# A rebuilt first chunk, and three smaller edits, in a gated attention and feed-forward kernel

## The chip, the cores and the metric

The kernel runs on one core of one Trainium2 chip. A core has TensorE (PE, matrix multiplication), VectorE (DVE), ScalarE (ACT), GpSimd (POOL) and SyncE (SP), each with its own instruction queue, and 16 DMA engines that all queues share. The metric is the device time of one execution in microseconds (us), lower is better. Times of a profile count from the start of its span.

## What is computed

```python
def _attn_ref(u, v, z):            # u, v: (8, 3008, 256)   z: (8, 3008, 64)
    scale = 1.0 / S
    scores = scale * np.matmul(z, z.transpose(0, 2, 1))
    attn = np.maximum(scores, 0.0) ** 2
    out = np.matmul(attn, v)
    return (u * out).astype(np.float32)

def _moe_ref(x, w_in, w_out):      # w_in: (256, 2048)   w_out: (2048, 256)
    h = x @ w_in
    g = h * (1.0 / (1.0 + np.exp(-1.702 * h)))
    return (g @ w_out).astype(np.float32)
```

The second function is applied to the 24064 rows that the first one gives. The scores are symmetric, since z is multiplied with itself.

## The kernel before

The eight batches are done one after the other. In a batch the 3008 rows of the sequence are six chunks of 512 (the last of 448), and a chunk is four blocks of 128; there are 24 blocks, NJ, numbered j. For each chunk i the loop of `attend` (L283) runs over all blocks j and multiplies V block j (stationary) with the squared scores of block j against chunk i (moving, 512 columns), for both halves c of V's columns, into two accumulators "o" in PSUM.

The scores come in units (i, jp) of two blocks: two matmuls of ZT with ZT (`scores`, L208), a relu by ScalarE out of PSUM to f16 "rl", a square by VectorE to "a" (`square`, L225). ZT is z transposed, with its 64 features twice on the 128 partitions, so that the two matmuls of a unit can run side by side in two halves of the array. Because the scores are symmetric, only units on and above the diagonal are worked out; for those below, "a" is turned by a DMA transpose on SP's queue into a tile "tt" (L253). Those of chunk 0 in batches 1 to 7 with jp 6 to 9 aren't turned at once: they go to a list `late`, which is worked off after unit (1, 11).

The order of all five engines is written out by hand: instructions stand in each engine's queue in the order in which the code emits them. `sched[i]` says at which step n of chunk i how many units are taken from `queue` (`take`, L591). After the attention of a batch come the up-projection (`up_group`, L348, "hg" and the gelu), the down-projection of four chunks as products of a seven-product scheme (`products` and `product`, L432 and L440, "st", with left sums "s" made by VectorE) and of two chunks plainly (`down64`, L505, "yp"). The next batch's chunk 0 units are taken in the two `down64` loops. In the last batch all six chunks use the seven-product scheme, and 14 products are left over after the last up-projection group.

The start of batch 0 is of its own kind (L599 to L616). V's first four blocks come on ACT's queue and all of z on SP's queue (`first_z`), then the rest of V on SP's. Seven matmuls on zeros warm TensorE up. z comes in six groups g of four blocks: VectorE casts a group to f16 twice, side by side (`first_cast`, L124), TensorE transposes it in four pieces into "zp" (`first_zt`, L130), and one engine copies it to ZT, ScalarE for g 0, 2 and 3 (L136), VectorE for the others (L138). Groups 2 to 5 are transposed at steps 2, 7, 13 and 21 of chunk 0. GpSimd casts V from f32 to f16 (L173) in two instructions for four blocks.

In chunk 0 of batch 0, step n stands for V half n % 2 of block n // 2 up to block 18; the last blocks follow per half. 14 units are taken up to its end: 12 of chunk 0 and two of chunk 1. A unit's PSUM tile "sc" has two buffers, "rl" three, "a" 21, "tt" 14 (shared with other tiles), the o and zp tiles together four.

Of the kernel before, what the change touches and what calls it, by code (L numbers as in the profile page):

```python
# [9 lines left out]
F32 = mybir.dt.float32  # L10
F16 = mybir.dt.float16
P = 128
# [3 lines left out]
def kernel(  # L16
# [25 lines left out]
    CB = CH // P  # L42
    NU = NJ // 2
# [30 lines left out]
    nil = pw.tile([P, CH], F16, name="nil", tag="gf")  # L74
    dve.memset(nil, 0.0)

    late = []
# [15 lines left out]
    def warm_up(n):  # L93

        w = ps1.tile([P, CH], F32, name="w", tag="ps1")
        for k in range(n):
            pe.matmul(w, nil[:, :P], nil, start=(k == 0), stop=(k == n - 1))  # L97

    def first_z(cuts):


        ZT[0] = pz.tile([P, NJ, P], F16, name="ZT", tag="ZT")
        ZT["st"] = [pa.tile([P, CB * CB, 2, DQK], F16, name="zst", tag="tt", bufs=14) for _ in range(2)]
        fs = [pw.tile([P, CB * CB, DQK], F32, name="zf", tag="y") for _ in range(2)]
        for n0, n1 in zip(cuts, cuts[1:]):
            zf = fs[n0 // (CB * CB)]
            m0 = n0 % (CB * CB)
            t0, last = n0 * P, n1 == NJ
            t1 = (n1 - CB if last else n1) * P
            sp.dma_start(  # L110
                zf[:, m0:m0 + (t1 - t0) // P, :].rearrange("p (g n) d -> p g (n d)", n=CB),
                z[0, t0:t1].rearrange("(g p n) d -> p g (n d)", p=P, n=CB),
            )
            if last:
                m1 = m0 + (t1 - t0) // P
                sp.dma_start(zf[:, m1:m1 + CB - 1, :], z[0, t1:S0].rearrange("(p n) d -> p n d", n=CB - 1))
                for h in range(2):
                    sp.dma_start(zf[h * SREM:(h + 1) * SREM, m1 + CB - 1, :], z[0, S0:S])
        ZT["f"] = fs

    def first_cast(g):
        m = g % CB * CB
        for c in range(2):
            dve.tensor_copy(ZT["st"][g // CB][:, m:m + CB, c, :], ZT["f"][g // CB][:, m:m + CB, :])  # L124

    def first_zt(g):
        z2 = ZT["st"][g // CB][:, g % CB * CB:(g % CB + 1) * CB]
        zp = ps1.tile([P, CB, P], F16, name="zp", tag="ps1")
        for k in range(CB):
            pe.transpose(zp[:, k, :], z2[:, k, :, :], ident)  # L130
        zt = ZT[0][:, g * CB:(g + 1) * CB, :].rearrange("d n p -> d (n p)")
        nb = CB if g < NCH - 1 else CB - 1
        dst = zt[:, :nb * P].rearrange("d (p n) -> d p n", n=nb)
        src = zp[:, :nb, :].rearrange("d n p -> d p n")
        if g in (0, 2, 3):
            act.activation(dst, src, AF.Copy, scale=1.0)  # L136
        else:
            dve.tensor_copy(dst, src)  # L138
        if nb < CB:
            dve.tensor_copy(zt[:, nb * P:], zp[:, nb, :])  # L140


    def load_z(b):
        ZT[b] = pz.tile([P, NJ, P], F16, name="ZT", tag="ZT")
# [12 lines left out]

    def load_v(b, n0, eng):


        if n0 == 0:
            V16[b] = pz.tile([P, NJ, NCC, P], F16, name="V16", tag="V16")
        if b or n0 < 3 * VB:
            vst = pu.tile([P, VB, D], F32, name="vst", tag="vst", bufs=3)
        else:
            vst = pa.tile([P, VB, D], F32, name="vst", tag="tt", bufs=14)
        full = min(VB, NJ - 1 - n0)
        eng.dma_start(vst[:, :full, :], v[b, n0 * P:(n0 + full) * P].rearrange("(n p) c -> p n c", p=P))
# [3 lines left out]
        for k in range(NCC):  # L172
            pool.tensor_copy(  # L173
                V16[b][:, n0:n0 + VB, k, :].rearrange("p n (q c) -> p n q c", c=QW),
                vst.rearrange("p n (q k c) -> p n q k c", k=NCC, c=QW)[:, :, :, k, :],
            )

    def width(i):
        return CH if i < NCH - 1 else LAST
# [43 lines left out]
        return [lambda u_=u_, sc=sc: square(b, *u_, sc) for u_, sc in zip(group, scs)]  # L223

    def square(b, i, jp, sc):  # L225
        rl = pw.tile([P, 2, CH], F16, name="rl", tag="rl", bufs=3)
        if folded(b, i) and jp == 2 * i + 1:
            rh = rl[:, :, :CH // 2]
            act.activation(rh, sc[:, :, :CH // 2], AF.Relu, scale=csc)
            dve.tensor_tensor(unit[b, i, jp][:, 1], rh, rh, ALU.mult)  # L230
            return
        act.activation(rl, sc, AF.Relu, scale=csc)  # L232
        if folded(b, i) and jp == 2 * i:
            a = pa.tile([P, CB, 2, P], F16, name="a", tag="a", bufs=21)
            unit[b, i, jp] = a
            r4 = rl.rearrange("p r (q c) -> p r q c", q=CB)
            dve.tensor_tensor(a.rearrange("p q r c -> p r q c"), r4, r4, ALU.mult)
            unit[b, i, jp + 1] = pa.tile([P, 2, 2, CH // 2], F16, name="ad", tag="a", bufs=21)
            sp.dma_start_transpose(
                unit[b, i, jp + 1][:, 0].rearrange("p g (r c) -> p (g r) c", c=P),  # L240
                a[:, CB // 2:].rearrange("p q r c -> p (q r c)"),
            )
            return
        a = pa.tile([P, 2, CH], F16, name="a", tag="a", bufs=21)
        unit[b, i, jp] = a
        dve.tensor_tensor(a, rl, rl, ALU.mult)  # L246
        cj = jp // 2
        if cj > i and (b or cj < NCH - 1):
            if (b, i, cj) not in TT:
                TT[b, i, cj] = pa.tile([P, CB, CB, P], F16, name="tt", tag="tt", bufs=14)  # L250
            k0 = 2 * (jp % 2)
            def turn_it():
                sp.dma_start_transpose(  # L253
                    TT[b, i, cj][:, k0:k0 + 2].rearrange("p r g c -> p (r g) c"),
                    a.rearrange("p r c -> p (r c)"),
                )


            if b and i == 0 and 6 <= jp < NU - 2:
                late.append(turn_it)  # L260
                return
            turn_it()
            while late and (i, jp) == (1, NU - 1):
                late.pop(0)()

    def weights(b, i, j):

# [283 lines left out]
    def split(lst, sizes):  # L551
# [24 lines left out]
    LOADW = {(3, NJ + 1): 0, (3, NJ + 11): 1, (4, 2): 2, (4, 10): 3, (5, 0): 4, (5, 6): 5, (5, 12): 6, (5, 18): 7}  # L576
    LOAD = {(3, NJ + 4): 4, (4, NJ + 5): 5}

    FIRST_ZT = {2: 2, 7: 3, 13: 4, 21: NCH - 1}
    SCHED0 = {  # L580
        0: {0: 1, 6: 2, 14: 2, 22: 2, 30: 2, 38: 2},
        1: {0: 2, 8: 2, 15: 2, 22: 2, 30: 2, 38: 2},
        2: {n: 1 for n in (0, 3, 7, 11, 30, 34, 38, 42)} | {NJ: 2},
        3: {n: 1 for n in (4, 9, 14, 19)} | {NJ: 2},
# [6 lines left out]
    def take(b, n):  # L591
        for post_ in scores(b, [queue.pop(0) for _ in range(n)]):
            post_()
# [15 lines left out]
    posts = scores(0, [queue.pop(0) for _ in range(2)])  # L609
    first_zt(1)  # L610
    posts[0]()
    first_cast(2)
    posts[1]()
    first_cast(3)
    take(0, 1)
    load_u(0, 1)  # L616

    for b in range(B):
# [3 lines left out]
        for i in range(NCH):  # L622
            for n, step in enumerate(attend(b, i, b == 0 and i < 2)):
                if b == 0 and i == 0 and n == 5:
                    load_u(0, 0)
                if b == 0 and i == 0 and n in FIRST_ZT:
                    first_zt(FIRST_ZT[n])
                    if 3 <= FIRST_ZT[n] < NCH - 1:
                        first_cast(FIRST_ZT[n] + 1)
# [12 lines left out]
        if more:  # L642
            for i in range(2):
                load_u(b + 1, i)
            load_z(b + 1)
            for n0 in range(0, NJ, VB):
                load_v(b + 1, n0, sp)
            fill(b + 1)
        prods = products(nst(b))
        for q in range(head, nup):  # L650
# [47 lines left out]
```

## Time and profile before

| | us |
|---|---|
| median of three runs (1203.95 to 1204.53) | 1204.45 |
| the profiled execution: its time | 1203.95 |
| its span | 1202.2 |
| mean of a relu, ScalarE, 128x1024 (L232) | 1.025 |
| mean of a square, VectorE, 128x1024 (L246) | 0.697 |
| mean of a V cast, GpSimd, 128x512 (L173) | 0.988 |
| a z cast, VectorE, 128x256 (L124), shortest and longest of 12 | 0.276 and 0.703 |
| a ZT copy, ScalarE (L136) and VectorE (L138), 128x512 | 0.60 and 0.69 |
| first o matmul | 8.54 |
| first scores in chunk 1 of batch 0 | 27.82 |
| TensorE's waits for a DMA transpose "tt", sum (two) | 1.2 |

A row of a timeline gives the start, the time until the last of its instructions ends, the engine, the line, the operation with its output and input tiles and shape, and the count; in brackets stands how long the engine was idle before, and what ended that. A row of the windows gives a stretch, its length, and the busy time of each engine in it. The clock is TensorE's, 1.00 for full speed. A wait by an engine that isn't the bound costs nothing.

### The profile page before, as it was taken

To read this page: it belongs to the slowest core of one execution; us is meant where nothing else is said; L and a number is where in the kernel's file an instruction comes from. 1 tells how busy PE (TensorE), PEld (TensorE's weight loads), DVE (VectorE), ACT (ScalarE), POOL (GpSimd) and SP (SyncE) were. 2 spreads that over 40 slices of the span, in tenths; PEclk is the share of its full clock that TensorE was granted. 3 is DMA by queue.
4 is the path that set the end of the run, shared out by engine and by line. 5 is a ranking of instruction groups with operands and counts; after the bars stand their busy time and mean duration, and the time that the engine had idled before them with its cause. 6 is when DMAs were issued, how large, how long until landed. Compare 5 with 4: busy or idle time off the path is not lost.

```text
span 1202.2 us, 28231 instructions
## 1 busy us (share of the span) xinstructions
PE 1192.0 (99%) x11785; PEld 723.3 (60%) x11785; DVE 830.6 (69%) x1277; ACT 770.2 (64%) x903; POOL 308.4 (26%) x363
## 2 busy tenths in 40 slices
PE   8999999999999999999999999999999999999998
PEld 2445765467654676546765467544775547855577
DVE  6669955597555976469654696638965489564886
ACT  6777684476844768366683666736677366772764
POOL 4144400462003520044200451015520145101000
PEclk9999999999999999999999999999999999999999
DMA  9966379562894639944399454984449854497012
GB/s 214 180 109 125 123 148 169 93 145 82 159 170 90 152 88 167 165 81 137 94 174 156 81 137 102 186 136 77 137 116 173 142 83 141 124 177 126 1 37 71
DMA packets 366592, 152.33 MB, mean 127 GB/s; under 512 B 313312, under 2 KB 358496, under 8 KB 366464
## 3 DMA queue, kind: packets, MB, share of 16 engines
q1 hardware_dynamic: 330320, 114.08, 48.3%
q0 software_dynamic: 35456, 35.86, 14.5%
q8 instruction: 92, 1.51, 0.5%
q10 hardware_dynamic: 688, 0.59, 0.2%
q14 instruction: 36, 0.29, 0.1%
HBM read 60.29 MB, written 24.64 MB: 71 GB/s over the span
## 4 chain that ended last, share of the span: by engine, by line
PE 97%; DVE 1%; DMA 1%; ACT 0%; issue 0%; ACTq 0%
PE o L314 38%; PE hg L355 27%; PE st L455 18%; PE yp L521 8%; PE sc L218 6%; DMA tt<-a 1%; DVE a L246 0%; PE w L97 0%; DVE gt L364 0%; DVE zst L124 0%; ACT gf L363 0%; DVE s L428 0%; PE zp L130 0%; ACT rl L232 0%; DVE s L426 0%
## 5 line engine op out<-in xcount | busy, mean ns | idle before, releaser
L363 ACT ACTIVATE gf<-hg 128x1024 f32<-128x1024 f32 (+1 forms) x384 | 385.7, 1007 | 164.4 <-PE hg L355 136.9
L232 ACT ACTIVATE rl<-sc 128x1024 f16<-128x1024 f32 x311 | 308.1, 1025 | 208.0 <-PE sc L218 206.0
L314 PEld LDWEIGHTS <-V 64*128 64x128 f16 (+1 forms) x4052 | 241.2, 94 | 243.4 <-issue 10.2
L355 PE MATMUL hg<-xt,W 128*128 128x512 f16 (+1 forms) x1408 | 354.5, 374 | 0.1
L364 DVE TENSOR_SCALAR gt<-gf 128x1024 f16<-128x1024 f32 (+1 forms) x384 | 275.8, 719 | 89.1 <-ACT gf L363 85.2
L246 DVE TENSOR_TENSOR a<-rl 128x1024 f16<-128x1024 f16 x276 | 192.0, 697 | 183.1 <-ACT rl L232 181.8
L314 PE MATMUL o<-a,V 64*128 64x512 f16 (+2 forms) x2010 | 318.3, 373 | 0.0
L188 POOL DMA_DIRECT2D uq<-in_u_dram x188 | 129.5, 696 | 512.6 <-PE sc L218 342.1
L314 PE MATMUL o<-tt,V 64*128 64x512 f16 (+1 forms) x1762 | 215.5, 376 | 1.3 <-DMA tt<-a 1.2
L355 PEld LDWEIGHTS <-W 128*128 128x128 f16 x1536 | 141.2, 98 | 117.4 <-issue 0.3
L455 PEld LDWEIGHTS <-gt 128*128 128x128 f16 x2176 | 132.4, 98 | 28.7
L218 PE MATMUL sc<-ZT 64*128 64x512 f16 (+1 forms) x692 | 122.3, 367 | 1.6 <-DVE ZT L138 0.8
L455 PEld LDWEIGHTS <-s 128*128 128x128 f16 x1632 | 99.2, 98 | 20.7
L173 POOL CAST V<-vst 128x512 f16<-128x512 f32 x96 | 91.1, 988 | 61.7 <-DMA vst<-in_v_dram 48.4
L521 PE MATMUL yp<-W,gt 64*128 64x256 f16 x1664 | 103.9, 269 | 0.0
L521 PEld LDWEIGHTS <-gt 64*128 64x128 f16 x1664 | 80.4, 94 | 19.2 <-POOLq L85 4.1
L331 DVE TENSOR_TENSOR xt<-o,ut 128x512 f16<-128x512 f32 x80 | 51.5, 685 | 38.1 <-PE o L314 38.1
L455 PE MATMUL st<-WT,gt 128*128 128x128 f16 x1088 | 71.8, 219 | 0.0
L455 PE MATMUL st<-W,gt 128*128 128x128 f16 x1088 | 71.7, 219 | 0.0
L455 PE MATMUL st<-WT,s 128*128 128x128 f16 x1088 | 71.5, 219 | 0.0
L465 ACT ACTIVATE uP<-st 128x256 f32<-128x256 f32 x102 | 39.1, 383 | 38.7 <-DVE y L471 33.7
L218 PEld LDWEIGHTS <-ZT 64*128 64x128 f16 x692 | 38.2, 94 | 37.6 <-issue 7.3
(47 smaller groups left out, 629.3 us busy)
## 6 DMA issues: line engine op xcount, KB each, us to landing
vst<-in_v_dram SPq DMA_DIRECT2D x39, 512.0 KB, 4.9
uq<-in_u_dram POOLq DMA_DIRECT2D x156, 128.0 KB, 3.5
out_dram<-y SPq DMA_DIRECT2D x33, 512.0 KB, 3.9
tt<-a SPq DMA_TRANSPOSE x230, 3.4
uq<-in_u_dram POOLq DMA_DIRECT2D x32, 112.0 KB, 2.9
out_dram<-y POOLq DMA_DIRECT2D x7, 512.0 KB, 4.9
vst<-in_v_dram SPq DMA_DIRECT2D x8, 384.0 KB, 4.6
out_dram<-y POOLq DMA_DIRECT2D x7, 384.0 KB, 3.2
```

Of the source, the lines that this page charges most:

```text
L173: pool.tensor_copy(V16[b][:, n0:n0 + VB, k, :].rearrange("p n (q c) -> p n q c", c=QW), vst.rearrange("p n (q k c) -> p n q k c", k=NCC, c ...
L188: eng.dma_start(uq[k * QW:(k + 1) * QW, :n // QW].rearrange("t q k c -> t q (k c)"), src[:, :, cs])
L218: pe.matmul(sc[:, r, :m * P], zt[h, 2 * kp + r, :], zt[h, (qi + 1) * CB - m:(qi + 1) * CB, :], start=True, stop=True,)
L232: act.activation(rl, sc, AF.Relu, scale=csc)
L246: dve.tensor_tensor(a, rl, rl, ALU.mult)
L314: ins = pe.matmul(acc[c][:, :n], V16[b][h, j, c, :], weights(b, i, j)[h], start=(k, m) == first[c], stop=(k, m) == final[c],)
L331: dve.tensor_tensor(x[:, c, :n], acc[c][:, :n], ut[:, :n], ALU.mult)
L355: pe.matmul(hg[:, e, :n], W1[:, c, ff * P:(ff + 1) * P], XT[b, i][:, c, :n], start=(c == 0), stop=(c == NCC - 1),)
L363: act.activation(gf[:, :, :n], hg[:, :, :n], AF.Gelu_apprx_sigmoid, scale=1.0 / FSC)
L364: dve.tensor_scalar(g, gf[:, :, :n], FSC, None, ALU.mult)
L455: pe.matmul(bank[:, m, :], lhs()[:, f, m, :], right[:, ff, :], start=name in ("P1", "P2", "P5") and m == 0 and ff == 0, stop=ff == NFF // ...
L521: ins = pe.matmul(yp[s // per][:, s % per, :], GT[b, k, ff // CB][h, ff % CB, s * P:(s + 1) * P], W2[h, ff, :], start=new, stop=n == last[ ...
```

## The change

The first chunk of batch 0 is written anew. z's first two groups are loaded by two queues (group 0 by SP, group 1 by ACT, ahead of V's first blocks), groups 2 and 3 by SP ahead of V's next blocks, groups 4 and 5 after these. A cast is now one instruction that reads its input twice. Group 0 is cast by GpSimd and VectorE, one half each, group 1 by VectorE, groups 2 to 5 by GpSimd, placed between the V casts, and V's first four blocks are cast block by block. Each copy to ZT is split: columns up to 64 of each block's row by ScalarE, the others by VectorE. The two warm-up matmuls between groups 0 and 1 are gone. The first two units, and units 2, 3, 5, 7 and 9, are relu'd and squared in halves of 512 columns; one relu half of units 1, 3, 5, 7 and 9 is made by VectorE. Units are taken two at a time at steps 7, 14, 21, 28 and 35 and one at step 42, together with the transposes of groups 3, 4 and 5 at the first three of these (before: one at step 0 and two at 6, 14, 22, 30 and 38).

Apart from the first chunk: the list `late` is gone, so that each unit is turned as soon as it is squared; the casts of later batches' V are called by the loop that loads it, in the same order; and in the loop over the leftover products two left sums stand ahead of each product, in place of one behind it.

```diff
-    def first_z(cuts):
...
+    def first_z(n0, n1, eng):
...
+    def first_cast(g, eng, c0=0, c1=2):
         m = g % CB * CB
-        for c in range(2):
-            dve.tensor_copy(ZT["st"][g // CB][:, m:m + CB, c, :], ZT["f"][g // CB][:, m:m + CB, :])
+        eng.tensor_copy(
+            ZT["st"][g // CB][:, m:m + CB, c0:c1],
+            ZT["f"][g // CB][:, m:m + CB].unsqueeze(2).to_broadcast([P, CB, c1 - c0, DQK]),
+        )
...
-        if g in (0, 2, 3):
-            act.activation(dst, src, AF.Copy, scale=1.0)
-        else:
-            dve.tensor_copy(dst, src)
-        if nb < CB:
-            dve.tensor_copy(zt[:, nb * P:], zp[:, nb, :])
+        def copies():
...
+            act.activation(dst[:, :SREM], src[:, :SREM], AF.Copy, scale=1.0)
+            dve.tensor_copy(dst[:, SREM:], src[:, SREM:])
+            if nb < CB:
+                dve.tensor_copy(zt[:, nb * P:], zp[:, nb, :])
+        return copies
+
+    def first_take(n, g=None):
+        posts = scores(0, [queue.pop(0) for _ in range(n)])
+        copies = first_zt(g) if g else None
+        posts[0]()
+        if g:
+            copies()
+        for post_ in posts[1:]:
+            post_()
+
+    def square_halves(jp, sc, r_dve):
+        rl = pw.tile([P, 2, CH], F16, name="rl", tag="rl", bufs=3)
+        a = unit[0, 0, jp] = pa.tile([P, 2, CH], F16, name="a", tag="a", bufs=21)
+        for r in range(2):
+            if r in r_dve:
+                dve.tensor_scalar(rl[:, r], sc[:, r], csc, 0.0, ALU.mult, ALU.max)
+            else:
+                act.activation(rl[:, r], sc[:, r], AF.Relu, scale=csc)
+        for r in range(2):
+            dve.tensor_tensor(a[:, r], rl[:, r], rl[:, r], ALU.mult)
+        turn_unit(0, 0, jp, a)
...
-            if b and i == 0 and 6 <= jp < NU - 2:
-                late.append(turn_it)
-                return
-            turn_it()
-            while late and (i, jp) == (1, NU - 1):
-                late.pop(0)()
...
-    FIRST_ZT = {2: 2, 7: 3, 13: 4, 21: NCH - 1}
+    FIRST = {7: (2, 3), 14: (2, 4), 21: (2, 5), 28: (2,), 35: (2,), 42: (1,)}
+    HALVES = {2: (), 3: (0,), 5: (0,), 7: (0,), 9: (0,)}
     SCHED0 = {
-        0: {0: 1, 6: 2, 14: 2, 22: 2, 30: 2, 38: 2},
+        0: {},
...
-    load_v(0, 0, act)
-    first_z((0, CB, 2 * CB, 4 * CB, NJ))
-    for n0 in range(VB, NJ, VB):
-        load_v(0, n0, sp)
+    first_z(0, CB, sp)
+    first_z(CB, 2 * CB, act)
+    casts = load_v(0, 0, act)
+    first_z(2 * CB, 4 * CB, sp)
+    for n0 in (VB, 2 * VB):
+        casts += load_v(0, n0, sp)
+    first_z(4 * CB, NJ, sp)
+    for n0 in range(3 * VB, NJ, VB):
+        casts += load_v(0, n0, sp)
+    first_cast(0, pool, 0, 1)
+    for n, cast in enumerate(casts):
+        if n in (0, 4, 8, 9):
+            first_cast((0, 4, 8, 9).index(n) + 2, pool)
+        cast()
     warm_up(7)
-    first_cast(0)
-    first_zt(0)
-    warm_up(2)
-    first_cast(1)
-    posts = scores(0, [queue.pop(0) for _ in range(2)])
-    first_zt(1)
-    posts[0]()
-    first_cast(2)
-    posts[1]()
-    first_cast(3)
-    take(0, 1)
+    first_cast(0, dve, 1, 2)
+    first_cast(1, dve)
+    for copies in [first_zt(g) for g in range(2)]:
+        copies()
...
+    copies = first_zt(2)
+    rls = [pw.tile([P, 2, CH], F16, name="rl", tag="rl", bufs=3) for _ in range(2)]
+    for k, r in ((0, 0), (0, 1), (1, 1)):
+        act.activation(rls[k][:, r], scs[k][:, r], AF.Relu, scale=csc)
+    dve.tensor_scalar(rls[1][:, 0], scs[1][:, 0], csc, 0.0, ALU.mult, ALU.max)
+    for k in range(2):
+        a = unit[0, 0, k] = pa.tile([P, 2, CH], F16, name="a", tag="a", bufs=21)
+        for r in range(2):
+            dve.tensor_tensor(a[:, r], rls[k][:, r], rls[k][:, r], ALU.mult)
+    copies()
+    first_take(1)
...
         for kp in prods:
+            for s_ in SUMS[:2]:
+                s_()
+            del SUMS[:2]
             product(b, *kp)
-            if SUMS:
-                SUMS.pop(0)()
```

More of the change, by code (lines that the diff above doesn't have):

```diff
@@ L75 @@
     dve.memset(nil, 0.0)
-    late = []
     ZT, V16, UQ, UT, XT, unit, TT = {}, {}, {}, {}, {}, {}, {}
@@ L97, in warm_up @@
             pe.matmul(w, nil[:, :P], nil, start=(k == 0), stop=(k == n - 1))
-    def first_z(cuts):
[L102 to L119, printed above, removed]
@@ L121, in first_cast @@
-    def first_cast(g):
+    def first_z(n0, n1, eng):
+        if 0 not in ZT:
+            ZT[0] = pz.tile([P, NJ, P], F16, name="ZT", tag="ZT")
+            ZT["st"] = [pa.tile([P, CB * CB, 2, DQK], F16, name="zst", tag="tt", bufs=14) for _ in range(2)]
+            ZT["f"] = [pw.tile([P, CB * CB, DQK], F32, name="zf", tag="y") for _ in range(2)]
+        zf = ZT["f"][n0 // (CB * CB)]
+        m0 = n0 % (CB * CB)
+        t0, last = n0 * P, n1 == NJ
+        t1 = (n1 - CB if last else n1) * P
+        eng.dma_start(
+            zf[:, m0:m0 + (t1 - t0) // P, :].rearrange("p (g n) d -> p g (n d)", n=CB),
+            z[0, t0:t1].rearrange("(g p n) d -> p g (n d)", p=P, n=CB),
+        )
+        if last:
+            m1 = m0 + (t1 - t0) // P
+            eng.dma_start(zf[:, m1:m1 + CB - 1, :], z[0, t1:S0].rearrange("(p n) d -> p n d", n=CB - 1))
+            for h in range(2):
+                eng.dma_start(zf[h * SREM:(h + 1) * SREM, m1 + CB - 1, :], z[0, S0:S])
@@ L122, in first_cast @@
+    def first_cast(g, eng, c0=0, c1=2):
         m = g % CB * CB
-        for c in range(2):
-            dve.tensor_copy(ZT["st"][g // CB][:, m:m + CB, c, :], ZT["f"][g // CB][:, m:m + CB, :])
+        eng.tensor_copy(
+            ZT["st"][g // CB][:, m:m + CB, c0:c1],
+            ZT["f"][g // CB][:, m:m + CB].unsqueeze(2).to_broadcast([P, CB, c1 - c0, DQK]),
+        )
     def first_zt(g):
@@ L130, in first_zt @@
             pe.transpose(zp[:, k, :], z2[:, k, :, :], ident)
[L131 to L134, printed above, removed]
-        if g in (0, 2, 3):
-            act.activation(dst, src, AF.Copy, scale=1.0)
-        else:
-            dve.tensor_copy(dst, src)
-        if nb < CB:
-            dve.tensor_copy(zt[:, nb * P:], zp[:, nb, :])
+        def copies():
+            zt = ZT[0][:, g * CB:(g + 1) * CB, :].rearrange("d n p -> d (n p)")
+            nb = CB if g < NCH - 1 else CB - 1
+            dst = zt[:, :nb * P].rearrange("d (p n) -> d p n", n=nb)
+            src = zp[:, :nb, :].rearrange("d n p -> d p n")
+            act.activation(dst[:, :SREM], src[:, :SREM], AF.Copy, scale=1.0)
[22 more added lines that the diff above has]
+        turn_unit(0, 0, jp, a)
     def load_z(b):
@@ L171, in load_v, with cast @@
                 eng.dma_start(vst[h * SREM:(h + 1) * SREM, full, :], v[b, S0:S])
-        for k in range(NCC):
+        def cast(k):
             pool.tensor_copy(
@@ L176, in load_v, with cast_block @@
             )
+        def cast_block(n):
+            pool.tensor_copy(
+                V16[b][:, n0 + n].rearrange("p k (q c) -> p k q c", c=QW),
+                vst[:, n].rearrange("p (q k c) -> p k q c", k=NCC, c=QW),
+            )
+        if b == n0 == 0:
+            return [lambda n=n: cast_block(n) for n in range(VB)]
+        return [lambda k=k: cast(k) for k in range(NCC)]
     def width(i):
@@ L225, in square @@
     def square(b, i, jp, sc):
+        if b == i == 0 and jp in HALVES:
+            square_halves(jp, sc, HALVES[jp])
+            return
         rl = pw.tile([P, 2, CH], F16, name="rl", tag="rl", bufs=3)
@@ L246, in square, with turn_unit @@
         dve.tensor_tensor(a, rl, rl, ALU.mult)
+        turn_unit(b, i, jp, a)
+    def turn_unit(b, i, jp, a):
         cj = jp // 2
@@ L251, in square @@
             k0 = 2 * (jp % 2)
[L252 to L256, printed above, removed]
-            if b and i == 0 and 6 <= jp < NU - 2:
-                late.append(turn_it)
-                return
-            turn_it()
-            while late and (i, jp) == (1, NU - 1):
-                late.pop(0)()
+            sp.dma_start_transpose(
+                TT[b, i, cj][:, k0:k0 + 2].rearrange("p r g c -> p (r g) c"),
+                a.rearrange("p r c -> p (r c)"),
+            )
     def weights(b, i, j):
@@ L599 @@
     fill(0)
-    load_v(0, 0, act)
-    first_z((0, CB, 2 * CB, 4 * CB, NJ))
-    for n0 in range(VB, NJ, VB):
-        load_v(0, n0, sp)
-    warm_up(7)
-    first_cast(0)
-    first_zt(0)
-    warm_up(2)
-    first_cast(1)
-    posts = scores(0, [queue.pop(0) for _ in range(2)])
-    first_zt(1)
-    posts[0]()
-    first_cast(2)
-    posts[1]()
-    first_cast(3)
-    take(0, 1)
+    first_z(0, CB, sp)
[12 more added lines that the diff above has]
+        cast()
+    warm_up(7)
+    first_cast(0, dve, 1, 2)
+    first_cast(1, dve)
+    for copies in [first_zt(g) for g in range(2)]:
+        copies()
+    scs = []
+    for k in range(2):
+        (i, jp), sc = queue.pop(0), ps2.tile([P, 2, CH], F32, name="sc", tag="ps2")
+        for r in range(2):
+            h = slice(r * DQK, (r + 1) * DQK)
+            pe.matmul(sc[:, r], ZT[0][h, 2 * jp + r, :], ZT[0][h, :CB, :], start=True, stop=True)
+        scs.append(sc)
+    copies = first_zt(2)
[3 more added lines that the diff above has]
+    dve.tensor_scalar(rls[1][:, 0], scs[1][:, 0], csc, 0.0, ALU.mult, ALU.max)
+    for k in range(2):
+        a = unit[0, 0, k] = pa.tile([P, 2, CH], F16, name="a", tag="a", bufs=21)
+        for r in range(2):
+            dve.tensor_tensor(a[:, r], rls[k][:, r], rls[k][:, r], ALU.mult)
+    copies()
+    first_take(1)
     load_u(0, 1)
@@ L625 @@
                     load_u(0, 0)
[L626 to L629, printed above, removed]
+                if b == 0 and i == 0 and n in FIRST:
+                    first_take(*FIRST[n])
                 if (i, n) in turn:
@@ L646 @@
             for n0 in range(0, NJ, VB):
-                load_v(b + 1, n0, sp)
+                for cast in load_v(b + 1, n0, sp):
+                    cast()
             fill(b + 1)
```

## The prediction

> **What bounds the kernel now.** I read the page's busy shares first, then the windows, then the first 30 us of the timeline engine by engine.
>
> ```profile
> span 1202.2 us, 28231 instructions
> ...
> PE 1192.0 (99%) x11785; PEld 723.3 (60%) x11785; DVE 830.6 (69%) x1277; ACT 770.2 (64%) x903; POOL 308.4 (26%) x363
> ```
>
> TensorE idles 10.2 us in all, so no edit can bring much more than that. The windows say where (columns: stretch, length, then busy time and count for PE, PEld, DVE, ACT, POOL, then clock, DMA share and GB/s):
>
> ```profile
> 0.00:4.40 4.40, 3.21 (x10) 1.12 (x11) 0.77 (x3) 1.28 (x1) 0.70 (x6) 1.00 0.52 154
> 4.40:16.00 11.60, 7.95 (x48) 2.84 (x46) 9.55 (x16) 7.39 (x9) 8.01 (x11) 1.00 1.08 309
> 16.00:150.00 134.00, 133.87 (x1115) 72.05 (x1115) 108.02 (x166) 96.89 (x108) 51.45 (x65) 0.99 0.74 136
> ...
> 1180.00:1202.20 22.20, 18.51 (x298) 16.92 (x295) 13.96 (x26) 7.60 (x14) 1.12 (x2) 0.98 0.24 74
> ```
>
> The idle time is 1.19 before the first warm-up, 3.65 between 4.4 and 16, about 1.5 over the 1164 us in the middle, and 3.69 at the very end, after the last matmul (output drain). Only the 3.65 is in reach, plus what it does to the clock. The PE rows and two half-microsecond windows:
>
> ```profile
> 8.54 0.60 PE L314 MATMUL o<-a,V 128*128 128x512 f16 x2
> 10.66 0.61 PE L218 MATMUL sc<-ZT 64*128 64x512 f16 x4 [0.43 <-ACT ZT L136]
> 11.65 1.46 PE L314 MATMUL o<-a,V 128*128 128x512 f16 x6
> 15.46 0.40 PE L130 MATMUL zp<-ident,zst 128*128 128x128 f16 x4 [2.36 <-DVE zst L124]
> 16.55 2.98 PE L314 MATMUL o<-a,V 128*128 128x512 f16 x7
> 20.82 1.90 PE L314 MATMUL o<-a,V 128*128 128x512 f16 x8
> 16.50:17.00 0.50, 0.50 (x4) 0.25 (x3) 0.50 (x2) 0.50 (x1) 0.50 (x2) 0.77 1.04 230
> 18.00:18.50 0.50, 0.50 (x3) 0.17 (x2) 0.28 (x2) 0.38 (x1) 0.50 (x2) 0.50 1.17 144
> ```
>
> TensorE waits 2.36 us at 13.1 for the VectorE cast of z group 4 (L124), then runs 7 matmuls in 2.98 us that warm take about 0.229 each. VectorE was late because its squares and GpSimd's V casts ran side by side (first row from the chain of waits, second from GpSimd's timeline):
>
> ```profile
> 12.15 2.02 DVE a L246 x2
> 9.17 7.88 POOL L173 CAST V<-vst 128x512 f16<-128x512 f32 x10 [2.81 <-DMA vst<-in_v_dram]
> ```
>
> A square takes 0.69 alone and 1.01 here; a cast 0.61 alone and up to 1.07 here.
>
> **What the skill says.** "TensorE: Matmul & The Clock Gate", Part 1: the clock halves or doubles after a free-running window of about 3.4 us according to how busy TensorE was. The trace agrees: the clock stood at 0.50 from about 16.7 to 20.2, 3.5 us, after the gap. "SBUF — State Buffer", section "SBUF: two separate sides": VectorE with two SBUF inputs and GpSimd share a port pair, and one blocks the other for the whole instruction. 0.69 to 1.01 and 0.61 to 1.07 agree. "VectorE: DVE Perf Modes", section on the TRN2 errata: every instruction pays a fixed cost, so halves cost more than half. Copies out of PSUM here took 0.69, 0.56 and 0.21 for 512, 384 and 128 elements: a slope of about 1.05 ns and 0.1 to 0.15 fixed. "DMA: Bandwidth & Descriptors", "Issuing engines are not separate DMA queues": a second queue saves only issue time. Agrees so far as the sum of both queues was 350 to 390 GB/s from 3.5 to 6.
>
> **The old first chunk in numbers.** From the first o matmul (8.54) to the first score of chunk 1 (27.82, so chunk 0 ends about 27.75) are 19.2 us. The warm work in it: 47 slots of o at 0.229 (8 in 1.83 on the chain) = 10.8; 10 units of scores at 0.27 (20.28 to 20.82 for two) = 2.7; 4 groups of transposes at 0.23 (8.98 to 9.20) = 0.9; sum 14.4. Lost: 0.43 + 2.36 idle, 3.5 us at half clock = 1.75, small gaps 0.3: 4.8.
>
> **The change, part by part.**
> *Loads.* z1 leaves on ACT's queue ahead of v0, z2 to z3 go ahead of v1 and v2. z0 and z1 (256 KB) land near 3.6; before, z1 was waited for until 5.46. v0 now shares with z2-3 and v1: I take 6.0 to 6.5 (5.13 before); z2-3 at 5.3. Both ACT and SP queues do little else here.
> *First o.* z0 is cast in two halves on two engines (0.28 on VectorE, about 0.4 on GpSimd). Transposes at 4.3, half copies of 0.39 (ScalarE: 0.60 for 512, 1.02 for 1024, so 0.82 ns each) and 0.42 (VectorE), scores near 5.45 in place of 5.57. The two warm-up matmuls go; they stood in waiting time, so they are worth 0, and the clock should still rise, since the window then is over 80% busy. First relu half at 6.1; VectorE does one half (0.69 out of PSUM, 6.6 to 7.3) and then four half squares at 0.42 (the 128x512 row of L230 took 0.42) with 0.2 each for the port, because V0 is cast in those microseconds. First half square ends 7.9, the fourth 9.7. So o starts near 7.95, gain 0.6, and slot 7 (n=6) ends at 10.0.
> *Groups.* From n=7 each group of seven slots has 1.6 of o, 0.54 of scores, 0.23 of transposes: 2.37 on TensorE. VectorE per group: relu half 0.69, two half squares 0.84, ZT half 0.42, a full square 0.69: 2.64, and while GpSimd casts about 0.7 more: 3.3. ScalarE: 0.39 + 0.60 + 1.02 = 2.0. So VectorE is the late engine for the three groups to n=27. GpSimd: from 5.4 casts of z2, four V0 blocks at 0.45, z3, V1, V2, z4, and so on at about 0.8 (7.88 for 10 before): z4 at 12.6, z5 14.5, V5 18.2.
> Walked in order: unit 3's first half square ends 12.3 (wait at n=12 0.3), unit 6's scores wait for ZT3 to 13.2, n=20 waits for unit 5 to 15.3, unit 8's scores wait for ZT4 to 16.2, unit 10's for ZT5 to 19.3 (0.7); n=41 ends 23.4, chunk 0 about 24.8. That is 7.95 + 14.4 + 2.45 of small waits. In none of these 3.4 us windows is TensorE under 60% busy, so I take no cold window; with one it is 1.75 more. Against 27.75: **3.0 us gained**.
> *u and stores.* SP's u load comes after one transpose instead of two, GpSimd's after V5, 1 us later than before (17.00); both are used after 22 us. Nothing.
> *The `late` list.* Four transposes per batch of b = 1 to 7 leave SP's queue after unit (1,11) and stand in the last tiles of the batch before. Count and bytes are unchanged, 28 are moved. SP rows of batch 4:
>
> ```profile
> 608.77 2.21 SPq L253 DMA_TRANSPOSE tt<-a  x1
> 614.11 1.22 SPq L239 DMA_TRANSPOSE ad<-a  x1
> 616.20 1.23 SPq L253 DMA_TRANSPOSE tt<-a  x1
> 628.30 1.69 PE L314 MATMUL o<-tt,V 64*128 64x512 f16 x14
> ```
>
> The queue is idle from 610.97 to 614.11 and 0.9 more before 616.20: 4.0 us. The four take 4 x 1.35 = 5.4. So what follows, ending with (1,11), comes 1.4 to 2 us later: it left at 621.2 to 622.5, now 624.5, landing 2.1 later (3.4 from issue start, 1.3 of it issue) at 626.6. Its reader is the fourth pair of the last row, 628.30 + 3 x 0.216 = 628.95. Slack 2.3: nothing. After (1,11) the queue is freer; nothing waited there but 1.2 us (662 and 787), not of these tiles. I take 0, ends -1 and +12.
> *Sums in pairs (last batch's tail).* VectorE does two left sums ahead of the product's y. y of the first product moves from 1187.48 to about 1189.0; its bank is wanted again at 1189.4. Nothing, at most 0.3.
>
> **Sum.** -3.0 against the profiled execution (1203.95, span 1202.2 and 1.75 around it): 1200.95. The median 1204.45 stands 0.5 above: **1201.4**.
>
> **Rivals.**
> *B, VectorE and GpSimd hardly collide*, since five relu halves and all ZT halves read PSUM. For it: copies from PSUM need not the pair. Against: squares did collide. Then o starts at 7.45 and small waits are 1.0: 22.85, gain 4.9: 1199.6.
> *C, GpSimd becomes the bound.* Four z casts are added to its twelve V casts. If every one took 1.07 (top of the row above) and V0's blocks 0.6: z2 6.5, V0 8.9, z3 10, V1 12.1, V2 14.2, z4 15.3, against 13.5 where TensorE wants it: 1.8, and a cold window 1.75 behind it. Gain -0.5: about 1204.6. For it: the casts between 10.6 and 13.6 did take 1.02 to 1.07. Against: the later ones took 0.62.
> *D, slower: the moved transposes pile up.* Beside an output store the transposes took 2.56 and 2.21 to issue (606.11, 608.77), and another store starts at 612.63. If the four and the five behind them take 1.9 each on average, (1,11) is out at 610.97 + 9 x 1.9 = 628.1 and lands at 630.2: 1.2 us of TensorE per batch, seven times, 8.4 less 3.0: 1209.8. It decides from 1.76 each (landing 628.95). Against: chunk 0 itself issues them at 1.35.
> *The change not doing what it says.* The rebuilt chunk takes 2 + 1 + 11 = 14 units up to the end of chunk 0, as before (3 + 11), so no score work is saved or moved out of it; what it can do is only to close gaps.
>
> **Chances.** Forecast 0.48, B 0.18, C 0.22, D 0.12. The forecast's own range is 1199.9 to 1202.9 (2.45 of waits between 1.0 and 4.0). A measurement of this kernel can tell about 0.2%, 2.4 us: faster is below 1202.04, slower above 1206.86. Faster: 0.38 of the forecast and B, 0.56; same: the rest of the forecast and C, 0.32; slower: D, 0.12. For 8 in 10: 1199.2 to 1205.0, which leaves out D and the lower part of B.
>
> **What would show it.** First o near 8.0; chunk 1's first scores near 24.9 in place of 27.82; no TensorE wait over 1 us before 25; clock 1.00 throughout; waits of TensorE on VectorE (squares, ZT), few on GpSimd. C shows as TensorE waiting for zst or V on GpSimd and a clock of 0.50. D shows as TensorE waiting for tt in chunk 1 of batches 1 to 7. The forecast is wrong if chunk 1 starts after 27 or before 23, or if tt waits grow beyond the 1.2 us.

## The result and the profile after

The changed kernel takes 1209.72 us (1207.88 to 1211.19, four runs) against 1204.20 (1202.00 to 1204.53, four runs) for the kernel before: ratio 1.0049, 95% interval 1.0028 to 1.0070. It is 5.9 us slower by that ratio, where 1201.4 was forecast. The profiled execution took 1210.98, with a span of 1209.1; its counterpart before had 1202.2.

The first two lines of the page show what did not happen:

```profile
span 1209.1 us, 28276 instructions
PE 1191.5 (99%) x11783; PEld 716.8 (59%) x11783; DVE 832.2 (69%) x1282; ACT 768.7 (64%) x908; POOL 311.1 (26%) x370
```

TensorE's busy time is what it was (1192.0 before); its idle time grew from 10.2 to 17.6 us. So nothing got more expensive for TensorE; it waits. The summary of TensorE's waits (line, what it waited for, sum in us, times, longest) says on what:

```profile
PE o L345 <- DMA tt<-a: 6.1, 4, 1.9
PE o L345 <- DVE a L667: 2.0, 3, 1.7
PE sc L252 <- ACT rl L269: 1.8, 3, 0.7
PE w L96 <- DVE nil L75: 1.2, 1, 1.2
PE st L486 <- ACT uP L496: 0.9, 1, 0.9
PE sc L657 <- DVE ZT L138: 0.7, 1, 0.7
```

The 2.36 us for zst, the cast of z, is gone, as intended. In its place stand three new kinds of wait: for squares and relus in the first chunk (L667, L269), for transposes "tt" (1.2 before, 6.1 now), and for uP, ScalarE's copy of a product, at the end. The windows of the same stretches as before (columns as before: PE, PEld, DVE, ACT, POOL, clock, DMA share, GB/s), with one half microsecond:

```profile
4.40:16.00 11.60, 8.19 (x44) 2.88 (x42) 9.04 (x15) 5.28 (x11) 10.44 (x18) 0.85 1.03 309
16.00:150.00 134.00, 132.02 (x1113) 71.62 (x1112) 109.36 (x170) 97.02 (x111) 50.52 (x64) 1.00 0.75 136
12.00:12.50 0.50, 0.50 (x4) 0.00 (x0) 0.50 (x2) 0.00 (x0) 0.50 (x2) 0.50 1.11 350
```

From 4.4 to 16, TensorE still loses 3.4 us, and its clock is at 0.50 in the middle of that stretch, where before it was at 0.50 some microseconds later. Up to 150 it loses 1.98 more (0.13 before). Where the waits of the first chunk come from is seen by laying TensorE, VectorE and ScalarE side by side (timelines):

```profile
9.15 1.25 PE L345 MATMUL o<-a,V 128*128 128x512 f16 x4 [1.71 <-DVE a L667]
18.92 0.39 PE L252 MATMUL sc<-ZT 64*128 64x512 f16 x2 [0.72 <-ACT rl L269]
25.00 0.39 PE L252 MATMUL sc<-ZT 64*128 64x512 f16 x2 [0.52 <-ACT rl L269]
28.46 0.60 PE L252 MATMUL sc<-ZT 64*128 64x512 f16 x4
...
7.53 0.69 DVE L663 TENSOR_SCALAR rl<-sc 128x512 f16<-128x512 f32 x1 [1.76 <-ACT rl L662]
8.13 3.12 DVE L667 TENSOR_TENSOR a<-rl 128x512 f16<-128x512 f16 x4
12.68 0.68 DVE L160 TENSOR_SCALAR rl<-sc 128x512 f16<-128x512 f32 x1
...
5.92 1.57 ACT L662 ACTIVATE rl<-sc 128x512 f16<-128x512 f32 x3 [0.66 <-PE sc L657]
13.45 0.60 ACT L162 ACTIVATE rl<-sc 128x512 f16<-128x512 f32 x1 [4.70 <-DVE rl L160]
17.08 0.60 ACT L162 ACTIVATE rl<-sc 128x512 f16<-128x512 f32 x1 [1.84 <-DVE rl L160]
```

Read the brackets. (A bracket names what ended an idle time, not what filled all of it: of the 4.70 us before 13.45, most passed before TensorE made those scores at 11.82.) VectorE's relu half of unit 1 (7.53) waits for ScalarE's half of the same score tile, and ScalarE's half of units 3 and 5 (13.45 and 17.08) waits for VectorE's half of the same tile. The two halves of a unit, meant to run side by side, run one after the other, and across two queues: ScalarE can't relu the second half until VectorE has got to the first, behind its copies and squares; the next full relu stands behind ScalarE's half; and TensorE waits for that relu (L269) because "sc" has only two buffers. Chunk 1 of batch 0 starts at 28.46, 0.64 later than before.

The sum: 0.64 at the start of chunk 1, 4.9 more of tt waits, 0.94 at the end (uP) are 6.5 of the 6.9 us by which the span grew. Not all of the 4.9 belongs to the moved transposes: one of the four tt waits, 1.42 us at 768.37, is in chunk 0 of batch 5, and two kernels below that keep `late` have a wait like it, of 1.68 and 1.50 us, near 765.5.

### The profile page after: what moved, and what is told of

Read it like the earlier page. It is cut to its first block, busy times and chain, and to the rows that moved or that the text cites. A ratio compares the mean times of both kernels' runs of the same rounds, so it can differ in the third digit from the quotient of the medians.

```text
span 1209.1 us, 28276 instructions
## 1 busy us (share of the span) xinstructions
PE 1191.5 (99%) x11783; PEld 716.8 (59%) x11783; DVE 832.2 (69%) x1282; ACT 768.7 (64%) x908; POOL 311.1 (26%) x370
## 4 chain that ended last, share of the span: by engine, by line
PE 94%; DMA 2%; DVE 2%; ACT 1%; issue 0%; ACTq 0%
PE o L345 37%; PE hg L386 26%; PE st L486 17%; PE yp L552 7%; PE sc L252 5%; DMA tt<-a 2%; ACT rl L269 1%; DVE gt L395 0%; DVE a L283 0%; PE w L96 0%; ACT gf L394 0%; DVE rl L160 0%; DVE a L667 0%; DVE s L457 0%; ACT rl L162 0%
## 5 line engine op out<-in xcount | busy, mean ns | idle before, releaser
L269 ACT ACTIVATE rl<-sc 128x1024 f16<-128x1024 f32 x304 | 301.5, 1026 | 206.0 <-PE sc L252 204.1
L345 PEld LDWEIGHTS <-V 64*128 64x128 f16 (+1 forms) x4052 | 235.0, 94 | 255.8 <-issue 10.8
L283 DVE TENSOR_TENSOR a<-rl 128x1024 f16<-128x1024 f16 x269 | 186.2, 693 | 187.2 <-ACT rl L269 184.8
```

Source lines behind the costliest of these rows:

```text
L345: ins = pe.matmul(acc[c][:, :n], V16[b][h, j, c, :], weights(b, i, j)[h], start=(k, m) == first[c], stop=(k, m) == final[c],)
```

## The experiments

All times of the runs are medians; ratios are to runs of the kernel before on the same chip, whose medians lay between 1204.2 and 1204.9.

### One part at a time

Three kernels each add one part of the change to the kernel before: the list `late` removed (first diff), the sums in pairs (second), the rebuilt first chunk with everything else put back (no diff; it is the large part of the change above).

```diff
-            if b and i == 0 and 6 <= jp < NU - 2:
-                late.append(turn_it)
-                return
             turn_it()
```

```diff
         for kp in prods:
+            for s_ in SUMS[:2]:
+                s_()
+            del SUMS[:2]
             product(b, *kp)
-            if SUMS:
-                SUMS.pop(0)()
```

> The kernel before with the list late taken out and nothing else. If the moved transposes are the cause of most of the loss: about 1209 us (1204.2 + 4.9), TensorE's waits for tt 4 to 8 us in all, in chunk 1 of several batches, first scores of chunk 1 of batch 0 still at 27.8. If they are harmless and the new waits for tt come from the first chunk's shift: 1204.2, waits for tt about 1.2 us.

> The kernel before with the two sums ahead of each leftover product and nothing else. If the pair makes ScalarE's copy of product P6 wait for VectorE's y: about 1205.1 us (+0.9), with a TensorE wait of some 0.9 us on ScalarE near the end. If the order of the sums doesn't matter: 1204.2 and no such wait.

> The changed kernel with the list late and the single sums put back: the rebuilt first chunk alone. If the three edits add up: about 1204.8 us (+0.6), first scores of chunk 1 of batch 0 near 28.5, waits for tt about 1.2 us. If the rebuilt chunk disturbs the later batches: 1207 or more with waits for tt in later batches.

| | median us (runs) | ratio and 95% interval |
|---|---|---|
| no list `late` | 1206.52 (22) | 1.0014 [1.0006, 1.0021] |
| sums in pairs | 1205.60 (22) | 1.0008 [1.0001, 1.0016] |
| rebuilt first chunk alone | 1206.32 (21) | 1.0013 [1.0007, 1.0020] |
| kernel before | 1204.38 (67) | 1 |

Each part alone costs something; the list `late`, expected to carry most of the loss (1209), carries 2.1. The medians add to 2.14 + 1.22 + 1.94 = 5.3 us, and 1209.72 less 1204.20 is 5.5, so no fourth part is needed to explain the change (by the ratios they add to 0.0035, 4.2 us, inside the changed kernel's interval of 3.4 to 8.4). None of the three is the gain that was forecast. The rebuilt chunk alone shows the same late starts as the changed kernel: first o at 9.50 and

```profile
28.95 0.61 PE L253 MATMUL sc<-ZT 64*128 64x512 f16 x4
```

as the first scores of chunk 1 (timeline of that run), with the clock at 0.50 from about 10 to 13.5.

### The rebuilt chunk with one reader for each PSUM tile

> As the rebuilt first chunk alone, but no PSUM tile is read by two engines: all relu halves by ScalarE, each copy to ZT whole on one engine. If the two engines' halves of one PSUM tile wait for each other and that chain (VectorE half, ScalarE half, next score tile) is what held the first chunk back: no wait of 1 us or more of TensorE after its first o matmul, first scores of chunk 1 near 25, about 1201.5 us. If GpSimd's casts beside VectorE's squares are the cause: the squares stay at 0.7 to 1.1 us each way, first scores of chunk 1 at 27 to 28.5, 1204 to 1205 us.

This kernel is the rebuilt chunk alone, with all relu halves on ScalarE and each copy to ZT whole on one engine. First o came at 7.41, chunk 1 at 24.10, 4.85 us earlier; the median was 1203.90 (14 runs), ratio 0.9998 [0.9985, 1.0011], where 1201.5 was expected. That is 1.8 us under the rebuilt chunk with split relus, so less than half of the 4.85 shows in the time; the two intervals leave 0 to 3.6, and where the rest went is not shown. It changes two things, so the next one changes only the relus:

```diff
-    HALVES = {2: (), 3: (0,), 5: (0,), 7: (0,), 9: (0,)}
+    HALVES = {2: (), 3: (), 5: (), 7: (), 9: ()}
...
-    for k, r in ((0, 0), (0, 1), (1, 1)):
+    for k, r in ((0, 0), (0, 1), (1, 0), (1, 1)):
...
-    dve.tensor_scalar(rls[1][:, 0], scs[1][:, 0], csc, 0.0, ALU.mult, ALU.max)
```

> As the kernel in which no PSUM tile is read by two engines, but with the copies to ZT split between ScalarE and VectorE again. If the split relu halves did the harm: first scores of chunk 1 of batch 0 at 24 to 25. If the split copies did: 27 or later, with TensorE waiting for ZT or for ScalarE's relu.

A single run took 1201.54, and the timeline of TensorE has chunk 1's first scores at 23.48:

```profile
7.61 1.97 PE L353 MATMUL o<-a,V 128*128 128x512 f16 x7
...
23.48 0.61 PE L253 MATMUL sc<-ZT 64*128 64x512 f16 x4
```

The same kernel in more runs:

> The same kernel as e8, timed in five rounds: the rebuilt first chunk without split relus, single sums, no early transposes. If the split relu alone spoiled the rebuilt chunk: chunk 1 of batch 0 starts at 23.5 to 24.5, the median is 1201 to 1202.5 (ratio 0.997 to 0.998), some 4 us under e3. If e8's single time was luck: chunk 1 still starts before 25, but the median is within 1 us of the kernel before, as e4's was.

1202.03 (21 runs), ratio 0.9984 [0.9974, 0.9995]: faster than before, and 3.5 us under the rebuilt chunk with split relus by the ratios (1.0013 - 0.9984 = 0.0029). The windows and timelines of this run (TensorE, ScalarE) beside those of the changed kernel:

```profile
4.40:16.00 11.60, 10.89 (x59) 4.41 (x58) 9.27 (x17) 8.64 (x17) 10.09 (x16) 1.00 1.12 308
...
8.15 2.71 PE L353 MATMUL o<-a,V 128*128 128x512 f16 x7
24.68 0.61 PE L253 MATMUL sc<-ZT 64*128 64x512 f16 x4
...
8.66 1.13 ACT L163 ACTIVATE rl<-sc 128x512 f16<-128x512 f32 x2
13.60 1.08 ACT L163 ACTIVATE rl<-sc 128x512 f16<-128x512 f32 x2
```

TensorE runs 59 instructions in the 11.60 us, where the changed kernel runs 44, and the clock column stays at 1.00. ScalarE makes five relu halves more in the chunk and is no later for it: two halves in 1.08 to 1.13 us without a break. The copies to ZT are still split here, and chunk 1 starts about as early as with whole copies, so the split copies did little harm. Yet they wait for each other too (VectorE's timeline in the single run above):

```profile
5.24 0.78 DVE L139 COPY ZT<-zp 128x256 f16<-128x256 f16 x2 [0.90 <-ACT ZT L138]
```

TensorE's first scores then come at 5.72 in that run, and at 5.47 with whole copies.

Last, the same edit made in the changed kernel itself, with its early transposes and pairs of sums left in:

> The changed kernel with one thing undone: both relu halves of a score tile are on ScalarE (as in e8). If the three costs add independently (early transposes 2.1, pairs of sums 1.2, the rest a first chunk that is 2.9 faster than before, as e10 was): the kernel before plus 0.4, median 1204.5 to 1206.5, ratio 0.9995 to 1.0015; chunk 1 of batch 0 starts at 23.5 to 25; tt waits of 2.5 to 6 us in chunk 1 and uP at 0.9 stay. If the transposes cost more the earlier the batches start (they meet the stores in every batch), the median stays at 1208 or more. If it falls to 1203 or less, the two other costs do not show once the first chunk is right.

1204.49 (14 runs), ratio 1.0009 [0.9997, 1.0022]; chunk 1 of batch 0 starts at 23.77. Moving VectorE's relu halves to ScalarE takes back 1.0049 - 1.0009 = 0.0040, 4.8 us, of the changed kernel's 5.9 us. What is left agrees with the sum of the other parts: +1.7 (transposes), +1.0 (sums), -1.9 (rebuilt chunk without split relus), each ratio times 1204.4, make +0.8, and +1.1 was measured. Its tt waits, 2.2 us in four, are fewer than the 6.1 of the changed kernel's profile with the same transposes, and than the 2.5 to 6 expected. This sum differs from one execution to another: the changed kernel's profile is of an execution of 1210.98, its second slowest, and this one of 1202.10, the fastest of 14; kernels that keep `late` and their stores show 0.6 to 3.2. So the 4.9 us above holds for that one execution, and the timed price of the part is 1.7.

### The early transposes and the output store

Which transposes wait, and beside what? Rows of SP's queue in batch 2 of the changed kernel (start, duration, line, count), then GpSimd's issues of output stores in the same microseconds, and the TensorE row that waited:

```profile
320.57 4.26 SPq L292 DMA_TRANSPOSE tt<-a  x1
326.29 2.20 SPq L276 DMA_TRANSPOSE ad<-a  x1
328.94 11.11 SPq L292 DMA_TRANSPOSE tt<-a  x8
...
318.57 0.76 POOL L528 DMA_DIRECT2D out_dram<-y  x1 [6.89 <-ACT y L565]
319.32 1.10 POOL L531 DMA_DIRECT2D out_dram<-y  x2
...
336.49 1.04 PE L345 MATMUL o<-tt,V 64*128 64x512 f16 x8 [1.44 <-DMA tt<-a]
484.62 1.04 PE L345 MATMUL o<-tt,V 64*128 64x512 f16 x8 [1.92 <-DMA tt<-a]
```

The four transposes that `late` used to hold back begin at 317.83 and the queue is free of them at 326.19: 8.4 us, with the store issued in the middle of them. The one issued just after the store takes 4.26. All that follows is late, up to unit (1, 11), issued at 333.19, whose reader in chunk 1 waits 1.44 us (batch 2) and 1.92 (batch 3). To show that it is the store, the next kernel takes the one without `late` and holds the stores of `down64` back until steps 32 and 40 of chunk 1 of the next batch (its recorded text says 31 and 39):

```diff
-                store(b, k, pool)
+                stores.append(lambda: store(b, k, pool))
...
+                if stores and i == 1 and n in (NJ + 8, NJ + 16):
+                    stores.pop(0)()
```

> The kernel before without the list late, and with the two output stores of the plain down-projection sent in chunk 1 of the next batch (steps 31 and 39), in place of beside the transposes. If it is the stores beside them that stretch the moved transposes: each transpose of that stretch issues in 1.3 to 1.5 us, no wait of TensorE for tt in chunk 1, about 1204.4 us or less. If four more transposes there are too many by themselves: about 1206.5 us and waits for tt in chunk 1 of some batches, as with the list taken out alone.

Batch 2's SP queue, first without `late` and with the stores in place, then with the stores held back:

```profile
305.03 19.18 SPq L253 DMA_TRANSPOSE tt<-a  x10
319.43 3.42 SPq L253 DMA_TRANSPOSE tt<-a  x1
319.43 4.78 SPq L253 DMA_TRANSPOSE tt<-a  x2
324.64 1.19 SPq L239 DMA_TRANSPOSE ad<-a  x1
```

```profile
304.52 15.34 SPq L253 DMA_TRANSPOSE tt<-a  x10
317.22 2.64 SPq L253 DMA_TRANSPOSE tt<-a  x2
320.27 1.19 SPq L239 DMA_TRANSPOSE ad<-a  x1
```

The ten transposes of chunk 0 take 15.34 us in place of 19.18. The ninth alone falls from 3.42 to 1.25 and the fifth, beside the other store, from 3.55 to 1.29. In these two profiles ad leaves 4.4 us earlier (0.5 of it because the batch itself is earlier), and no chunk 1 has a tt wait any more (four had without `late`). The median is 1204.61 (13 runs), ratio 1.0002 [0.9990, 1.0014]: the part's cost is gone or nearly so, though the interval reaches that of the run with the stores in place (1.0014).

> The rebuilt first chunk with no PSUM tile read by two engines and full relus and squares from unit 2 on, the list late kept, sums as before, and the two output stores in chunk 1 of the next batch. If the first chunk now gains what it was to gain (first scores of chunk 1 of batch 0 near 24) and the waits for tt in chunk 0 come from the stores: 1200 to 1201 us. If the gain of the first chunk is given back later: 1203.5 or more.

This one was meant to beat both and did the opposite: 1232.45 (5 runs), ratio 1.0231. It keeps `late` and holds the stores back. The transposes of the list are issued in chunk 1 too, in one block, and now the held-back stores stand beside that block (SP and GpSimd in batch 2, the waiting TensorE row, and the sum over the run):

```profile
326.88 20.22 SPq L296 DMA_TRANSPOSE tt<-a  x12
347.20 2.14 SPq L279 DMA_TRANSPOSE ad<-a  x1
...
341.98 1.53 POOL L538 DMA_DIRECT2D out_dram<-y  x2 [44.28 <-ACT rl L272]
343.50 1.09 POOL L541 DMA_DIRECT2D out_dram<-y  x2
...
351.28 0.61 PE L355 MATMUL o<-ad,V 64*128 64x512 f16 x4 [2.73 <-DMA ad<-a]
...
PE o L355 <- DMA ad<-a: 22.0, 7, 4.3
```

and the same block in the kernel before:

```profile
321.49 17.07 SPq L253 DMA_TRANSPOSE tt<-a  x12
```

Twelve transposes take 20.22 us here and 17.07 in the kernel before; the last of them, issued at 343.24 beside the store, takes 3.85. Chunk 2's ad comes late, and TensorE waits for it once in each of batches 1 to 7. What I had overlooked is that the slack for a held-back store had been spent by `late`. Its failure is the same mechanism once more: a store costs where it stands beside transposes that are due soon.

### The sums

> The kernel before with two sums behind each leftover product, in place of one. If it is the place of the pair (ahead of VectorE's y) that costs: no wait of st on ScalarE's uP near the end, the last 15 us as before. If the pair itself costs: the same wait of 0.9 us.

A single run took 1204.95, which alone decides nothing about the time. The wait at the end stays, 0.77 us where the pair ahead of each product had 0.94; here are the timelines of this run (ScalarE, TensorE):

```profile
1193.46 0.38 ACT L465 ACTIVATE uP<-st 128x256 f32<-128x256 f32 x1 [3.49 <-DVE y L471]
1193.89 1.95 PE L455 MATMUL st<-WT,s 128*128 128x128 f16 x32 [0.77 <-ACT uP L465]
```

So it is not the place but the pairing. ScalarE copies a product's bank into uP, VectorE reads uP into y, and uP has one buffer for each of the three products of a chunk that are copied so. With two sums per product VectorE needs 2 x 0.64 + 0.42 = 1.7 us for a product that ends in a y, in place of 1.06, while TensorE needs 0.9; so the y that frees uP slips, ScalarE's next copy waits 3.49 us for it (1.50 in the kernel before), and TensorE waits to go on in the bank that this copy reads.

### Both repairs together

The kernel without split relus, with single sums, without the list `late`, and with the stores held back:

> The rebuilt first chunk with the relu halves of a score tile all on ScalarE (as in e8), single sums, no early transposes for chunk 1, and the output stores of the ZU product moved to steps 32 and 40 of chunk 1 of the next batch. If the first chunk's gain and the uncovered transposes are independent: chunk 1 of batch 0 starts near 23.5 to 24.5, TensorE waits for tt in no chunk 1, tt waits in all under 2 us, median 1200.0 to 1201.8, ratio 0.996 to 0.998. If the gain of the first chunk is given back later (batch 0 meets its next transposes earlier, or other waits take the place): chunk 1 starts as early, but the median is 1203.5 or more. If the moved stores collide as in e6: TensorE waits for ad of chunk 2 in most batches and the median is over 1215.

The words "no early transposes" in that text are wrong: in this kernel, as in the one with held-back stores above, each unit is turned at once. It took 1201.55 (19 runs), ratio 0.9978 [0.9968, 0.9989], 2.6 us under the kernel before by the ratio, and the fastest that was timed; chunk 1 of batch 0 starts at 24.39 and no chunk 1 waits for tt (2.5 us of tt waits remain where under 2 was expected, 1.78 of them at 216.57, in a later chunk of batch 1). It is 0.5 us under the one with `late` kept (1202.03), which these runs can't tell from nothing.

## Why the prediction was wrong

**The direction.** The forecast was a gain of 3.0 us with everything else at nothing. The rebuilt chunk lost, and both edits put at nothing cost something. Two of the forecast's own signs of being wrong came: chunk 1 started after 27, and the tt waits grew. By timed parts it is 1.6 us for the rebuilt chunk, 1.7 for the transposes and 1.0 for the sums.

**The step that failed: "VectorE per group: relu half 0.69, two half squares 0.84 ... ScalarE: 0.39 + 0.60 + 1.02".** This walked each engine's load by itself and let the two halves of a score tile go side by side. The traces show each half waiting for the other engine's half of the same tile. With the halves on one engine, chunk 1 starts at 23.48 and 24.68 (one kernel, two executions) and at 23.77; with them split at 28.46 and 28.95. The forecast's 24.9 for this row lies near the kernels without split relus, but it was reckoned for halves side by side, which no run here has. By the timed pairs that change only this, the step is worth 3.5 us (the rebuilt chunk alone; the two intervals leave some 2 to 5) to 4.8 us (the changed kernel; some 2 to 8). Moving the halves also frees VectorE of five times 0.69 us, so these runs do not part the waiting from VectorE's load. For the waiting speak the brackets: VectorE itself stood idle 1.76 us for ScalarE's half before 7.53, and the first o matmul waited 1.71 us behind it. The two engines also write a half each of the tile rl, but that a shared SBUF tile makes them wait is not seen: group 0's cast is split the same way over the SBUF tile zst, and there GpSimd's half (3.46 to 3.98) and VectorE's (3.43 to 3.72) run together in the changed kernel. The tiles that two engines read where they wait, sc and zp, are in PSUM.

The Trainium skill has a warning near this: "PSUM — Partial Sum Buffer", section "PSUM bank collisions raise a hardware error", says that a compiler adds a dependency between two engines' accesses to one bank, reads too. The traces agree in so far as the dependency is there. The same section lets engines work in different banks at once, and by the page's bank size (2 KiB per partition) a half of 512 f32 is a bank of its own; so the wait seen here is probably the program's, which tracks the tile as a whole, not the memory's. A version with two separate PSUM tiles for the halves, which would also part the waiting from the load, was not tried, so this last point is argued only.

**"First half square ends 7.9, the fourth 9.7", so o at 7.95.** It was 9.15. VectorE's half relu began at 7.53 in place of 6.6, and the four half squares took 3.12 us, 0.78 each, where 0.62 was taken. In the single run of the rebuilt chunk without split relus they began at 6.78, beside GpSimd's casts of 128x256 (four in 1.81 us), and took 2.38, 0.60 each, near the price. In the changed kernel they came at 8.13, beside casts of 128x512 all through (four in 2.86). That the larger casts hold them up longer agrees with the port pair which the prediction cited; no run here moved the casts alone.

**"I take no cold window."** The clock stood at 0.50 from about 11.0 to 14.4. The walk had no 1.7 us wait for squares and so had TensorE busy enough. In the 3.4 us before the clock fell TensorE was busy for 1.63 us here and for 1.37 in the rebuilt chunk alone (1.24 in the kernel before). The cold stretch thus seems to follow from the failed step: the clock column shows none in the runs without split relus. The walk's line of 60% is not measured by any run; these stretches were 48% and 40% busy.

**"The four take 4 x 1.35 = 5.4 ... Slack 2.3: nothing."** They took 8.4 beside the store, in the one batch that was laid out above. Rival D had the mechanism right, from SP rows of 2.56 and 2.21 beside a store in the kernel before, and even the place (tt in chunk 1, reader of (1, 11)). Only its size was off: it charged 1.2 us in every one of seven batches, 8.4; the changed kernel's profile has 1.44, 1.92 and 1.29 us in chunk 1 of batches 2, 3 and 7 (and 1.42 in chunk 0 of batch 5), and the timed cost is 1.7. The argument against it, "chunk 0 itself issues them at 1.35", used rows that no store stood beside. That D's 1209.8 lies on the measured median is chance: it carried the first chunk as a gain of 3.0.

**"Its bank is wanted again at 1189.4. Nothing, at most 0.3."** It was 0.9. The y moved about as reckoned (to 1188.7 on the old time scale, where 1189.0 was forecast), but I had followed the PSUM bank and not uP, the one-deep buffer between the bank and VectorE's y.

**What was right.** The size of the old gap and that it closes: the 2.36 us for zst is gone, and GpSimd is named in none of TensorE's waits in the changed kernel. That fells rival C for this kernel: the casts of the first 17 us took 0.6 to 0.8, not 1.07. (Its own sum should read 1204.95, not 1204.6.) With the relus put right some casts do take 1.06, and in the fastest kernel TensorE waits 0.72 us for GpSimd's zst and 0.36 for its V. Rival B (hardly any collision) falls by the 0.60 to 0.78 of a half square. The u loads and the shared queues cost nothing that shows.

## What to carry to other kernels

Before splitting one PSUM tile between two engines, look whether the program lets both read at once; if each waits for the other's half, both queues are tied together, and the cost is the longer queue's delay, not half an instruction. Before calling a moved transfer free, lay the other queues' large transfers over its new place: a price taken from undisturbed rows doesn't hold there, and neither does the slack if something else has been moved into it. For every stage that gets later, follow all buffers between producer and reader, the small one-deep ones first.

## What was not expected of the hardware

A transpose issued beside an output store took 3.42 to 4.26 us on SP's queue, and the one of 3.42 took 1.25 when that store was moved. The store's own issue on GpSimd takes only 0.76 and 1.10, so a glance at GpSimd's busy time hides it.

The same kernel without split relus, profiled twice, had its first seven o matmuls in 1.97 and in 2.71 us, with the clock shown as 1.00 over both stretches, and its chunk 1 at 23.48 and 24.68: 1.2 us of the first 25 differ between executions with nothing changed. That is two fifths of what the forecast hoped for, so a single run of each kernel could not decide it.
